# A spectral block with a gated feed-forward: lower parts and first block reordered, no moves on GpSimd's queue, second bias by a transfer

## The chip, the core and the metric

The kernel runs on one core of a Trainium2 chip. TensorE (PE) multiplies, VectorE (DVE), ScalarE (ACT) and GpSimd (POOL) work on tiles, and transfers between the chip's memory and the on-chip memory are issued by SyncE (SP) or by the queues of ACT and POOL. Each engine works through its own instructions in program order and waits where an operand isn't ready. The metric is the device time of one execution in microseconds (us); lower is better.

## What is computed

One token sequence of 4096 rows with 640 channels goes through two residual parts. In the first, a layer norm and a modulation (`sa`, `ca`, `ga`, taken from `silu(c) @ w_mod`) are followed by a real two-dimensional Fourier transform over the sequence, a two-layer block-diagonal complex network on the frequencies, a soft threshold, and the inverse transform. In the second part, a layer norm and a modulation are followed by a gated feed-forward network.

```python
    h = _layernorm(x, axis=-1) * (1 + ca) + sa
    x = x + ga * _A_ref(h, A_w1, A_b1, A_w2, A_b2)
    h = _layernorm(x, axis=-1) * (1 + cb) + sb
    x = x + gb * _B_ref(h, B_w_gate, B_w_up, B_w_down)
```

and in `_A_ref`, per frequency and for each of four blocks of 160 channels:

```python
        hr = jnp.einsum('bhwni,nio->bhwno', zr, w1[0]) - jnp.einsum('bhwni,nio->bhwno', zi, w1[1]) + b1[0]
        hi = jnp.einsum('bhwni,nio->bhwno', zi, w1[0]) + jnp.einsum('bhwni,nio->bhwno', zr, w1[1]) + b1[1]
        hr = hr * (lambda x, dt: x.astype(dt))(hr > 0, x.dtype)
...
        or_ = jnp.einsum('bhwni,nio->bhwno', hr, w2[0]) - jnp.einsum('bhwni,nio->bhwno', hi, w2[1]) + b2[0]
...
        or_ = jnp.sign(or_) * mr * (lambda x, dt: x.astype(dt))(mr > 0, x.dtype)
```

## The kernel before

The sequence is seen as 128 x 32 rows. Eight tiles `xa0` to `xa7` hold four of the 32 columns each (128 partitions x 4 x 640 numbers, 1280 KB).

**The first stage** is a loop over the tiles. `ln_stats` and `ln_apply` normalise a tile on DVE, POOL and ACT; `dft_a` (line 432) multiplies it by a 128 x 128 Fourier matrix on PE, in five matmuls `i` = 0 to 4 (the fifth takes the last 32 channels of each block); `evac_a` (line 442) copies the five results back over `xa`, on ACT, and in the last two tiles `i` = 1 and 3 on DVE; `moves` (line 366) issues what follows the tile: `write_s1(t, f)` writes the frequencies of group `f` of tile `t` to a scratch in memory, from where `load_g(ch, us)` reads a chunk of frequencies of all tiles, turned. Eight chunks `ch` are worked on one after the other. For the first chunk tiles 6 and 7 don't go through memory: `move_g(0, t, i, queue)` (line 314) moves 40 KB of row block `i` straight into the chunk's tile `g0`; `i` = 0, 1 are issued by POOL and `i` = 2, 3 by SP (lines 394 and 398). A move reads whole rows, so it needs the copy `i` and the copy of the fifth result, which comes last.

**Numbers are kept in two parts.** Matmuls run in a shortened format; a factor is split into a rounded upper part (`weights_high`, `evac_rh`, the ACT line of `evac_b`) and the rest, the lower part (`weights_low`, `evac_rl`, the DVE line of `evac_b`). `prep_weights` lists the jobs for a weight tensor: for `w1` twelve (`prep1`), of which 0, 1, 2 belong to the first 128 output columns, 6, 7, 8 to the second 128, and 3, 4, 5, 9, 10, 11 to the remaining 32 of both; for `w2` six (`prep2`, reordered in line 524).

**Between the first stage and the chunks** (lines 475 to 489): `columns` makes the modulation's columns, `ca1` is taken from it on DVE; the second bias `b2` is brought to all partitions by three matmuls (six in the trace) of ones with `b2s`, a tile that holds the bias in its first row and zeros elsewhere, and three ACT copies to `b2t`; `idle(4)` issues matmuls that nothing reads; ACT makes the upper parts of jobs 6 to 11, and DVE the lower parts of all twelve. SP then has in its queue (lines 492 to 504): the second half of the raw `w2`, eight writes to the scratch, `load_g(1)` in four pieces, `load_tb(1)`, ten more writes (tile 4 first), and small constants.

**The chunks** have four blocks `b` each. `stage_b(ch, t)` (line 594) finishes the transform with four small matmuls (eight in the trace), `evac_b` and `evac_r` scale the result by `ca1` and split it into `z` and `rz`. `stage_l1(ch, b)` (line 646) is the first layer: groups `o` = 0, `o` = 1 and a third of 32-column parts, each reading `z`, `rz` and upper and lower `w1`. `stage_l2` (line 695) is the second layer, in two halves `q`; its result gets the bias from `b2t` on DVE on its way to `tts` (line 713). A loop over positions `p` = 4·`ch` + `b` (line 837) writes the order of all of this by hand, so that the queues of the engines are fixed. Before the loop (lines 792 to 805) stand `stage_b` for (0,0), (0,4) and (0,1), the upper parts 1 and 0 of `prep2` on ACT, `evac_b` and `evac_r` of blocks 0 and 1, and the rest of `prep2`: a lower part on DVE and five operations on POOL.

**Memory.** Pool `sp` (raw `w1`, `wm1`, `b2s`, `acc0`) is left after the lower parts, and pool `hp` (`rz`, `h32`, `h`, ...) takes its place. Pool `xp` (the eight `xa`) is left after the last write is queued, and pool `p2` takes its place. `xp` holds the tiles in the order 1, 2, 3, 0, 4, 5, 6, 7 with 10,240 bytes per partition each; `p2` ends at the same edge and is one such tile longer, so that `w2b` lies where `xa1` was, `w2c` where `xa2` was, `tts` of odd chunks where `xa0` was, and `tts` of even chunks where `xa4` was. A first write there waits until the old tile has been read.

**The second part** of the kernel, the feed-forward network, follows from line 1067. Its order is made by a planner at build time from fixed costs; the change doesn't touch it.

Of the kernel before, what the change touches and what calls it, by code (L numbers as in the profile page):

```python
# [9 lines left out]
OP = mybir.AluOpType  # L10
# [163 lines left out]
def body(tc, x, w1, b1, w2, b2, wg, wu, wd, c, wm, k_fa, k_tb, k_tx, k_bm, k_bx, k_ga, k_ge, k_id, out, dbg=None):  # L174
# [27 lines left out]
    with ExitStack() as top:  # L202
# [35 lines left out]
        with ExitStack() as af:  # L238
# [97 lines left out]
            stx = ExitStack()  # L336
            xp = stx.enter_context(tc.tile_pool(name="xp", bufs=1, side="right"))
            rp = af.enter_context(tc.tile_pool(name="rp", bufs=1))
            b2t = rp.tile([P, 2, NB, BS], F32, name="b2t")
            with tc.tile_pool(name="sp", bufs=1) as sp:  # L340
                xas = []
                xts = {t: xp.tile([P, 4, D], F32, name=f"xa{t}") for t in (1, 2, 3, 0, 4, 5, 6, 7)}

                def load_x(t):
                    xa = xts[t]
                    if t < 3:
                        for i in range(4):
                            nc.sync.dma_start(xa[:, i, :], xv[:, 4 * t + i, :])
                    else:
                        nc.sync.dma_start(xa, xv[:, 4 * t:4 * t + 4, :])  # L350
                    xas.append(xa)


                def write_s1(t, f):
                    nc.sync.dma_start(s1[f][4 * t:4 * t + 4].rearrange("n r d -> r n d"),
                                      xas[t][(slice(0, 64, 4), slice(64, P, 4), slice(2, P, 4), slice(1, P, 2))[f]])

                for t in range(6):
                    load_x(t)
                wm1 = sp.tile([P, 5, D], F32, name="wm1")  # L360
                stats = {}
                pas = {}
                raws = {}


                def moves(t):
                    if t < 6:
                        write_s1(t, 0)
                    if t < 4:
                        write_s1(t, 1)  # L370
                    if t == 0:
                        load_x(6)
                        nc.sync.dma_start(c5, c)
                    elif t == 1:
                        load_x(7)
                        raws[1] = load_weights(sp, w1, "1")
                    elif t == 2:
                        nc.sync.dma_start(wm1, wm[:, 1])
                    elif t == 3:
                        load_tb(0)  # L380
                        nc.sync.dma_start(b1m, b1[:, 0:8].rearrange("p (r b) -> p r b", r=2))
                        nc.sync.dma_start(b1r, b1[0:64, 8:12])
                        nc.sync.dma_start(b2s[0:1], b2.rearrange("r b o -> (r b o)").unsqueeze(0))
                    elif t == 4:

                        load_g(0, (0, 1))
                        raws[2] = load_weights(rp, w2, "2", (0,))
                    elif t == 5:
                        for f in (2, 3):
                            write_s1(1, f)  # L390
                    elif t == 6:

                        for i in range(4):
                            move_g(0, t, i, (pool, nc.sync)[i // 2])
                        load_g(0, (2,))
                    elif t == 7:
                        for i in range(4):
                            move_g(0, t, i, (pool, nc.sync)[i // 2])


                def ln_stats(t):
                    n = 1 if t < 2 else 4
                    for i in range(0, 4, n):
                        mv, rs = layer_stats(lp, xas[t][:, i:i + n, :], n, f"a{t}_{i}")
                        nm = lp.tile([P, 4], F32, tag="nm", bufs=7, name=f"nm{t}_{i}")
                        pool.tensor_tensor(nm[:, :n], mv[:, :, 0], rs, op=OP.mult)
                        pool.tensor_tensor(nm[:, :n], nm[:, :n], mone[:, :n], op=OP.mult)
                        for k in range(n):
                            stats[t, i + k] = (mv[:, k, 0:1], rs[:, k:k + 1], nm[:, k:k + 1])

                def ln_apply(t):
                    xa = xas[t]
                    for i in range(4):
                        mean, rs, nm = stats[t, i]
                        if i >= (4, 2, 2, 3, 2, 3, 2, 1)[t]:
                            dve.tensor_scalar(xa[:, i, :], xa[:, i, :], mean, rs, op0=OP.subtract, op1=OP.mult)
                        else:
                            act.activation(xa[:, i, :], xa[:, i, :], AF.Identity, bias=nm, scale=rs)


                b2s = sp.tile([P, 2 * NB * BS], F32, name="b2s")
                pool.memset(b2s, 0.0)
                acc0 = sp.tile([P, D], F32, name="acc0")
                wx0 = sp.tile([P, P], F32, name="wx0")

                def first_scale(lo, hi):
                    if lo == 0:
                        dve.tensor_scalar(acc0, wm1[:, 0, :], sc[:, 0:1], None, op0=OP.mult)
                    for k in range(max(lo, 1), hi):
                        dve.scalar_tensor_tensor(acc0, wm1[:, k, :], sc[:, k:k + 1], acc0, op0=OP.mult, op1=OP.add)  # L430

                def dft_a(t):

                    xnr = xas[t].rearrange("p a (b e) -> p a b e", b=NB)
                    for n, i in enumerate((0, 1, 2, 3, 4) if t < 7 else (4, 0, 1, 2, 3)):
                        j = 5 * t + n
                        pa = (bank0(j // 4, [P, 512], f"pa{t}_{i}") if j % 4 == 0
                              else ps.tile([P, 512], F32, tag=f"p{j % 4}", name=f"pa{t}_{i}"))
                        mm(pa, fa, xnr[:, i, :, 0:128] if i < 4 else xnr[:, :, :, 128:160], start=True, stop=True)
                        pas[t, i] = pa  # L440

                def evac_a(t):
                    xa = xas[t]
                    for i in range(5):
                        if t > 5 and i % 2:
                            dve.tensor_copy(xa[:, i, 0:512], pas[t, i])
                        elif i == 4:
                            act.activation(xa[:, :, 512:640], pas[t, i].rearrange("p (a e) -> p a e", a=4), AF.Copy)
                        else:
                            act.activation(xa[:, i, 0:512], pas[t, i], AF.Copy)  # L450

                ln_stats(0)
                ln_stats(1)
                ln_apply(0)
                for t in range(8):
                    if t + 2 < 8:
                        ln_stats(t + 2)
                    if t + 1 < 8:
                        ln_apply(t + 1)
                    dft_a(t)  # L460
                    if t == 6:

                        prep1 = prep_weights(raws[1], w1a, w1b, w1c, True)
                        for job in prep1[:6]:
                            weights_high(*job, pool)
                        first_scale(0, 2)
                    evac_a(t)
                    if t == 6:
                        first_scale(2, 5)
                        remainders(acc0, wx0)  # L470
                    if t == 2:
                        act.activation(sc, c5, AF.Silu)
                    moves(t)

                pm1 = columns(acc0, wx0)
# [7 lines left out]
                for job in prep1[6:]:  # L483
                    weights_high(*job)
                b2v = b2t.rearrange("p r b o -> p (r b o)")
                for n, w in enumerate((512, 512, 256)):
                    act.activation(b2v[:, 512 * n:512 * n + w], pbs2[n][:, :w], AF.Copy)
                for job in prep1:
                    weights_low(*job)
# [3 lines left out]
            for t in (2, 3):  # L493
                for f in (2, 3):
                    write_s1(t, f)
# [2043 lines left out]
```

## Time and profile before

| | us |
|---|---|
| median of three runs | 1414.55 |
| lowest and highest run | 1413.67, 1416.0 |
| the profiled execution | 1411.32 |
| its span, first to last instruction | 1409.5 |

The profile is of one execution. A timeline row gives start and duration, the engine, the line of the program, the tiles written and read, how many instructions are taken together, and in brackets how long the engine sat idle before and what ended it; SPq rows are transfers issued, not their movement. PEld is the loading of a matmul's weights, which overlaps PE. A row of windows gives for each stretch of time its length and each engine's busy time with its count, then the granted clock, the busy share of the DMA engines and the data rate. A row of transfers gives how many, the KB of each, and the median time from issue to landing where the trace has it.

### The profile page before, as it was taken

How to read it: one execution, taken by the hardware profiler on the slowest of the kernel's cores; microseconds unless marked ns; L12 is line 12 of the kernel's file. 1: busy time of each engine (PE TensorE's matmuls, PEld its weight loads, DVE VectorE, ACT ScalarE, POOL GpSimd, SP SyncE). 2: the span in 40 equal slices, each digit the busy share in tenths (PEclk: the TensorE clock that was granted, in tenths of full speed). 3: DMA queues.
4: the chain of work that ended last, by engine and by line, in shares of the span. 5: the costliest groups of instructions: out<-in, count | busy, mean ns of one | idle time of the engine just before them, and what ended most of it. 6: DMA issues, size and time to landing. Idle time of an engine off the chain costs nothing. (4 is left out here: it accounts for less than half of the span.)

```text
span 1409.5 us, 23754 instructions
## 1 busy us (share of the span) xinstructions
PE 1382.5 (98%) x8410; PEld 1310.7 (93%) x8410; DVE 1067.8 (76%) x1861; ACT 765.0 (54%) x1542; POOL 604.6 (43%) x683
## 2 busy tenths in 40 slices
PE   6899999999999999999999999999999999999998
PEld 2599999967999889899999999999999999999998
DVE  8889888889888888649787668678678757375644
ACT  6879999755555554436454345546164624262341
POOL 5700200157766594326445534447153624042241
PEclk9999999999999999999999999999999999999999
DMA  9876466675998897898877998696998668956634
GB/s 371 310 244 211 157 196 193 203 232 170 327 353 308 308 335 263 293 368 308 308 225 281 375 330 288 236 326 230 375 330 309 217 218 282 350 194 217 199 115 149
DMA packets 171016, 377.34 MB, mean 268 GB/s; under 512 B 22193, under 2 KB 81649, under 8 KB 168882
## 3 DMA queue, kind: packets, MB, share of 16 engines
q1 hardware_dynamic: 161794, 359.28, 73.6%
q0 software_dynamic: 6800, 13.93, 3.1%
q10 hardware_dynamic: 2304, 2.62, 0.5%
q8 instruction: 66, 1.08, 0.3%
q14 instruction: 52, 0.43, 0.1%
HBM read 269.48 MB, written 96.80 MB: 260 GB/s over the span
## 5 line engine op out<-in xcount | busy, mean ns | idle before, releaser
L1442 DVE TENSOR_TENSOR wb<-r,wb 128x768 fp32r<-128x768 f32 (+3 forms) x170 | 170.4, 1013 | 13.5 <-ACT wb L1435 13.3
L2050 PE MATMUL pw<-h,wt 128*128 128x384 f32 x412 | 139.3, 338 | 0.6 <-ACT s_y L2069 0.6
L2052 PE MATMUL pw<-h,wt 128*128 128x384 f32 x412 | 138.3, 336 | 0.0
L2051 PE MATMUL pw<-h,wt 128*128 128x384 f32 x412 | 138.1, 335 | 0.0
L1435 ACT ACTIVATE wb<-r 128x768 fp32r<-128x768 f32 (+3 forms) x168 | 104.5, 639 | 56.3 <-PE pw L2063 41.7
L2351 PE MATMUL pc<-wq,L 128*128 128x320 f32 x846 | 132.7, 309 | 0.9 <-DMA wq<-wqd 0.9
L2110 POOL TENSOR_TENSOR sg<-s_x,sg 128x384 f32<-128x384 f32 x24 | 30.0, 1250 | 234.5 <-DVE s_x L2076 234.5
L2351 PEld LDWEIGHTS pc<-wq,L 128*128 128x128 f32 x846 | 126.3, 188 | 1.1 <-DVE x L2308 1.1
L2130 DVE TENSOR_TENSOR L<-sg,L 128x384 fp32r<-128x384 f32 x144 | 101.0, 725 | 27.7 <-ACT L L2126 27.2
L2069 ACT ACTIVATE s_x<-pw 128x384 f32<-128x384 f32 x52 | 25.6, 492 | 164.2 <-PE pw L2052 162.3
L2050 PE MATMUL pw<-h,wb 128*128 128x384 f32 x312 | 105.0, 336 | 0.0
L2051 PE MATMUL pw<-h,wb 128*128 128x384 f32 x312 | 104.4, 335 | 0.0
L2052 PE MATMUL pw<-h,wb 128*128 128x384 f32 x312 | 104.4, 335 | 0.0
L2121 POOL TENSOR_TENSOR sg<-sg,sg 128x384 f32<-128x384 f32 x72 | 91.9, 1276 | 23.4 <-DVE L L2130 20.0
L1973 PE MATMUL pg<-ht,wb 128*128 128x512 f32 x260 | 101.8, 392 | 0.0
L2351 PE MATMUL pe<-wq,L 128*128 128x320 f32 x648 | 101.7, 309 | 0.0
L1974 PE MATMUL pg<-ht,wb 128*128 128x512 f32 x260 | 101.3, 390 | 0.0
L1975 PE MATMUL pg<-ht,wb 128*128 128x512 f32 x260 | 101.2, 389 | 0.0
L2267 PE MATMUL pd<-wq,a 128*128 128x320 f32 x632 | 96.8, 310 | 0.0
L2351 PEld LDWEIGHTS pe<-wq,L 128*128 128x128 f32 x648 | 96.6, 188 | 0.0
L2267 PEld LDWEIGHTS pd<-wq,a 128*128 128x128 f32 x632 | 93.5, 188 | 0.5
L772 POOL DMA_DIRECT2D s<-co x28 | 15.7, 559 | 175.9 <-ACT co L771 175.9
(317 smaller groups left out, 3914.1 us busy)
## 6 DMA issues: line engine op xcount, KB each, us to landing
wq<-wqd SPq DMA_DIRECT2D x83, 640.0 KB, 6.1
wt<-td SPq DMA_DIRECT2D x103, 512.0 KB, 5.4
hs<-ho SPq DMA_DIRECT2D x52, 512.0 KB, 5.2
h<-hs SPq DMA_DIRECT2D x32, 768.0 KB, 7.9
td<-wt SPq DMA_DIRECT2D x25, 512.0 KB, 6.3
r<-in_B_w_gate_dram SPq DMA_DIRECT2D x24, 384.0 KB, 4.4
r<-in_B_w_up_dram SPq DMA_DIRECT2D x24, 384.0 KB, 4.3
xx<-tt SPq DMA_DIRECT2D x56, 160.0 KB, 3.3
```

The source lines that it names most:

```text
L1435: def high(ks, e=slice(0, c), copy=lambda o, i: act.activation(o, i, AF.Copy)):
L1442: dve.tensor_tensor(wbs[t, n][:, 1, ks, e], raw[t, n][:, ks, e], f32(wbs[t, n][:, 0, ks, e]), op=OP.subtract)
L1973: mm(b, wh, hh, start=(kk == 0), stop=False)
L1974: mm(b, wh, hl, start=False, stop=False)
L1975: mm(b, wl, hh, start=False, stop=(kk == 4))
L2050: mm(b, w(0, kp), a[:, kp, 0], start=start and kp == 0, stop=False, skip_group_check=not start)
L2051: mm(b, w(0, kp), a[:, kp, 1], start=False, stop=False, skip_group_check=not start)
L2052: mm(b, w(1, kp), a[:, kp, 0], start=False, stop=kp == 1, skip_group_check=not start)
L2121: pool.tensor_tensor(o, x, y, op=op)
L2130: dve.tensor_tensor(o[:, 1], raws[j], f32(o[:, 0]), op=OP.subtract)
L2267: mm(b[:, :320], l, m, start=start and i == 0, stop=stop and i == len(s) - 1)
L2351: mm(o[:, :320], ls[q][:, x, k], w[:, q, y], start=start and q == 0 and n == 0, stop=q == 1 and n == 2, skip_group_check=not start)
```

## The change

Five edits, all between the end of the first stage and the first positions of the loop.

1. **Moves.** Tiles 6 and 7 are moved by SP alone, except that `i` = 0 and 2 of tile 7 are issued by ACT. The moves stand ahead of the other transfers of their step.
2. **Raw weights.** The first half of the raw `w2` is loaded in step 5, behind the scratch writes of that step, in place of step 4.
3. **Copies of tile 7.** Only `i` = 3 stays on DVE; `i` = 1 goes to ACT.
4. **Second bias.** `b2s`, its memset, its load, its matmuls and its ACT copies go. One transfer reads the bias for each of the 128 partitions (640 KB written), behind `load_tb(1)` in SP's queue. `idle(4)` becomes `idle(6)`.
5. **Lower parts.** DVE makes the lower parts 0 to 5, then `ca1`, then (behind the definitions that are moved up) part 6, the lower parts of `z` and `rz` of block 0, then parts 7 to 11, and only then those of block 1. `rz` moves from pool `hp` to pool `lp`, as it's now written while `sp` is still in use.

```diff
                 def moves(t):
                     if t < 6:
                         write_s1(t, 0)
+                    else:
+                        for i in range(4):
+                            move_g(0, t, i, nc.scalar if t == 7 and i % 2 == 0 else nc.sync)
...
-                        nc.sync.dma_start(b2s[0:1], b2.rearrange("r b o -> (r b o)").unsqueeze(0))
                     elif t == 4:
                         load_g(0, (0, 1))
-                        raws[2] = load_weights(rp, w2, "2", (0,))
                     elif t == 5:
                         for f in (2, 3):
                             write_s1(1, f)
+                        raws[2] = load_weights(rp, w2, "2", (0,))
                     elif t == 6:
-                        for i in range(4):
-                            move_g(0, t, i, (pool, nc.sync)[i // 2])
                         load_g(0, (2,))
-                    elif t == 7:
-                        for i in range(4):
-                            move_g(0, t, i, (pool, nc.sync)[i // 2])
...
-                        if t > 5 and i % 2:
+                        if t == 6 and i % 2 or t == 7 and i == 3:
                             dve.tensor_copy(xa[:, i, 0:512], pas[t, i])
...
                 pm1 = columns(acc0, wx0)
-                dve.tensor_scalar(ca1, pm1[:, 0:5], 1.0, None, op0=OP.add)
-                pbs2 = []
-                for n, w in enumerate((512, 512, 256)):
-                    pbs2.append(ps.tile([P, 512], F32, tag="p2" if n else "p1", name=f"pb2_{n}"))
-                    mm(pbs2[n][:, :w], ones, b2s[:, 512 * n:512 * n + w], start=True, stop=True)
-                idle(4)
+                idle(6)
                 for job in prep1[6:]:
                     weights_high(*job)
-                b2v = b2t.rearrange("p r b o -> p (r b o)")
-                for n, w in enumerate((512, 512, 256)):
-                    act.activation(b2v[:, 512 * n:512 * n + w], pbs2[n][:, :w], AF.Copy)
-                for job in prep1:
+                for job in prep1[:6]:
                     weights_low(*job)
+                dve.tensor_scalar(ca1, pm1[:, 0:5], 1.0, None, op0=OP.add)
...
                 load_tb(1)
+                nc.sync.dma_start(b2t.rearrange("p r b o -> p (r b o)"),
+                                  b2.rearrange("r b o -> (r b o)").unsqueeze(0).to_broadcast([P, 2 * NB * BS]))
                 for t in (4, 0, 5, 6, 7):
                     write_s1(t, 2)
...
+                for b, tag in ((0, None), (4, None), (1, "p2")):
+                    stage_b(0, b, tag)
+                for n in (1, 0):
+                    weights_high(*prep2[n])
+                weights_low(*prep1[6])
+                evac_b(0, 0)
+                evac_r(0, 0)
+                for job in prep1[7:]:
+                    weights_low(*job)
...
+            evac_b(0, 1)
+            evac_r(0, 1)
+            weights_low(*prep2[0])
+            weights_rest(1)
+            for n in (2, 3):
+                weights_high(*prep2[n], pool)
...
-                    rzs[ch] = hp.tile([P, NB, 258], F32R, tag="rz", bufs=2, name=f"rz{ch}")
+                    rzs[ch] = lp.tile([P, NB, 258], F32R, tag="rz", bufs=2, name=f"rz{ch}")
```

The rest of the diff moves definitions and the issue of the same transfers to an earlier place in the program, in the same order.

More of the change, by code (lines that the diff above doesn't have):

```diff
@@ L506, in body @@
-            stx.close()
-            nc.sync.dma_start(idn, k_id)
-            nc.sync.dma_start(tx, k_tx)
-            p2 = af.enter_context(tc.tile_pool(name="p2", bufs=1, side="right", reuse_waits="tile"))
-            w2a = p2.tile([P, NB, 640], F32R, name="w2a")
-            w2b = p2.tile([P, NB, 640], F32R, name="w2b")
-            w2c = p2.tile([P, NB, 640], F32R, name="w2c")
-            acc = p2.tile([P, D], F32, name="acc")
-            cl = p2.tile([P, D], F32, name="cl")
-            wx = p2.tile([P, P], F32, name="wx")
@@ L518, in body @@
-            bx = p2.tile([P, 2, 128], F32, name="bx")
-            wmts = {(0, 1): p2.tile([P, D], F32, tag="wn", bufs=1, name="wm0_1")}
-            p2.tile([P, 256], F32, name="gap")
-            tts = {(1, q): p2.tile([P, 2, D], F32, tag="tu", bufs=2, name=f"tt1_{q}") for q in range(2)}
-            prep2 = prep_weights(raws[2], w2a, w2b, w2c, False)
-            prep2 = [prep2[i] for i in (0, 3, 1, 4, 2, 5)]
-            def weights_rest(n):
-                w, h, l, v, _ = prep2[n]
-                pool.tensor_tensor(w[:, :, l], v, f32(w[:, :, h]), op=OP.subtract)
@@ new lines, in body, with load_e @@
+            et = None
+            NP = 4 * NCH
+            LAST = NP - 4
+            def load_e():
+                nonlocal et
+                et = fx.tile([P, 4, D], F32, tag="gx", bufs=2, name="et")
+                nc.sync.dma_start(et.rearrange("p a b -> p (a b)"), k_ge.rearrange("p a b -> p (a b)"))
+            evac_b(0, 1)
[4 more added lines that the diff above has]
+                weights_high(*prep2[n], pool)
```

377 lines of the change are left out of this document (188 added, 189 removed).

## The prediction

> **What bounds the kernel now.** I read the page's head first, then the table of windows over the stretch that the change touches. The rows in each fence are picked from their views, not neighbours there.
>
> ```profile
> span 1409.5 us, 23754 instructions
> 55.80:60.20 4.40, 3.85 (x32) 3.70 (x33) 2.65 (x8) 2.63 (x5) 4.40 (x3) 1.00 0.95 378
> 60.20:75.40 15.20, 12.85 (x101) 12.20 (x101) 14.64 (x25) 11.47 (x26) 7.90 (x7) 1.00 0.98 361
> 75.40:262.00 186.60, 186.46 (x1456) 185.21 (x1454) 163.01 (x317) 172.68 (x355) 17.51 (x52) 1.00 0.60 193
> ```
>
> The columns of busy time are PE, PEld, DVE, ACT, POOL. From 75.4 us on PE is busy for 186.46 of 186.60 us, so whatever time PE's work there is moved by should reach the end of the kernel. From 60.2 to 75.4 it isn't PE: DVE is busy for 14.64 of 15.20 us. The start of this stretch and its end are found among PE's waits between 54 and 80 us:
>
> ```profile
> PE pb L600 <- DMA g<-xa: 1.4, 1, 1.4
> PE pc L711 <- DVE r L691: 1.1, 1, 1.1
> PE pc L711 <- DVE w2c L286: 0.5, 1, 0.5
> ```
>
> So there are two gates. The first stage_b waits for the moves, and the first second-layer block waits for DVE, whose last piece is the lower part of `w2c`. The change works on the first gate and lengthens, in part, the DVE queue that leads to the second.
>
> **First gate: the moves.** Rows of the timeline of SP, POOL, ACT, DVE and PE, and the issue-to-landing rows of single transfers (a write of tile 5, `load_g` of piece 2, the last two moves of POOL, and the page's small transfers):
>
> ```profile
> 43.67 1.95 SPq L355 DMA_DIRECT2D s<-xa  x3
> 46.65 1.61 SPq L316 DMA_DIRECT2D g<-xa  x2
> 50.14 0.53 SPq L311 DMA_DIRECT2D g<-s  x1
> 50.76 1.20 SPq L316 DMA_DIRECT2D g<-xa  x2
> 50.23 1.13 POOL L316 DMA_DIRECT2D g<-xa  x2 [0.30 <-ACT xa L448]
> 49.34 0.60 ACT L448 ACTIVATE xa<-pa 128x512 f32<-128x512 f32 x1 [0.26 <-PE pa L439]
> 49.21 1.28 DVE L446 COPY xa<-pa 128x512 f32<-128x512 f32 x2
> 55.84 2.36 PE L600 MATMUL pb<-tb,g 128*128 128x128 f32 x19 [1.43 <-DMA g<-xa]
> s<-xa SPq DMA_DIRECT2D x1, 160.0 KB, 6.4
> g<-s SPq DMA_DIRECT2D x1, 320.0 KB, 5.2
> g<-xa POOLq DMA_DIRECT2D x2, 40.0 KB, 4.8
> xx<-tt SPq DMA_DIRECT2D x56, 160.0 KB, 3.3
> ```
>
> POOL's last move is issued at about 50.23 + 1.13/2 = 50.8 and lands 4.8 later, at 55.6; PE starts at 55.84. Piece 2 of `g0` is close behind: 50.14 + 5.2 = 55.3. It's issued so late because it reads what tile 5 wrote, and that write, issued at 43.67 behind 640 KB of raw weights, lands at 43.67 + 6.4 = 50.1.
>
> With the raw weights behind it, the write of tile 5 no longer sets that time. SP issues four moves of tile 6 from 46.65 (two took 1.61, so to about 49.7 with slack in between, 49.4 without), then piece 2 at 49.4 instead of 50.14. Its landing is 49.4 + 5.2 = 54.6 with its own latency, 52.7 with the 3.3 of the small transfers. The last copy of tile 7 still ends at 49.34 + 0.60 = 49.94. DVE now has one of the two copies of 0.64, done at 49.9 too. Behind that ACT and SP issue two moves each (0.60 apiece from SP's 1.20): the last one starts at 50.6 and lands between 50.6 + 3.3 = 53.9 and 50.6 + 4.8 = 55.4. I take 54.6, where piece 2 with its own row and the middle of the moves agree. With the 0.2 from landing to PE as before, stage_b starts at 54.8: **1.0 earlier**, bounds 0.2 and 1.7.
>
> The Trainium skill (DMA: Bandwidth & Descriptors, "Issuing engines are not separate DMA queues") says that transfers of all issuing engines run on the same 16 DMA engines, and that issuing from several saves the issue time alone. By that rule the 4.8 would stay, the gain would be the 0.2 above, and this is rival C.
>
> **Second gate: DVE's queue.** What ACT, DVE and POOL do from there:
>
> ```profile
> 49.83 0.62 ACT L283 ACTIVATE w1a<-rm 128x512 fp32r<-128x512 f32 x1
> 51.79 0.30 ACT L283 ACTIVATE w1c<-rr 128x128 fp32r<-128x128 f32 x1
> 53.88 1.36 ACT L283 ACTIVATE w2a<-rm 128x640 fp32r<-128x640 f32 x2
> 54.53 0.69 DVE L286 SCALAR_TENSOR_TENSOR w1b<-rm,w1b 128x512 fp32r<-128x512 f32 x1
> 56.14 0.28 DVE L286 SCALAR_TENSOR_TENSOR w1c<-rr,w1c 128x128 fp32r<-128x128 f32 x1
> 57.73 0.75 DVE L608 SCALAR_TENSOR_TENSOR z<-pb,ca,z 128x512 fp32r<-128x512 f32 x1 [1.31 <-ACT z L607]
> 60.85 0.98 DVE L640 SCALAR_TENSOR_TENSOR rz<-pb,ca,rz 32x256 fp32r<-32x256 f32 x2 [0.23 <-ACT rz L630]
> 61.86 1.83 DVE L286 SCALAR_TENSOR_TENSOR w2a<-rm,w2a 128x640 fp32r<-128x640 f32 x1
> 65.98 1.69 DVE L286 SCALAR_TENSOR_TENSOR w2b<-rm,w2b 128x640 fp32r<-128x640 f32 x1
> 69.16 0.89 DVE L286 SCALAR_TENSOR_TENSOR w2c<-rr,sgn,w2c 128x640 fp32r<-128x640 f32 x1
> 54.71 3.11 POOL L528 TENSOR_TENSOR w2a<-rm,w2a 128x640 fp32r<-128x640 f32 x1 [3.35 <-ACT w2a L283]
> 57.80 3.59 POOL L281 TENSOR_SCALAR w2b<-rm 128x640 fp32r<-128x640 f32 x2
> 61.47 1.54 POOL L528 TENSOR_TENSOR w2b<-rm,w2b 128x640 fp32r<-128x640 f32 x1
> 65.45 1.53 POOL L528 TENSOR_TENSOR w2c<-rr,w2c 128x640 fp32r<-128x640 f32 x1
> ```
>
> *Lower parts moved.* Parts 7 to 11 ran from 54.53 to 56.42 (1.9) while DVE had time: it then waited 1.31 for `z`. Now they stand behind `rz` of block 0, in the stretch where DVE is the bound. They cost 1.9 there, less the 0.23 that DVE waited before `rz` of block 1: **1.65 later**. DVE's free time before `z` grows and isn't used. The first layer doesn't wait for them: its second group comes about 1 us after the first, in which parts 7 and 8 are made.
>
> *POOL and DVE in each other's way.* The same form, 128x640 with two operands from on-chip memory, took 1.83 and 1.69 while POOL ran its own two-operand form (61.47 to 63.0 and 65.45 to 67.0), and 0.89 with POOL free. POOL's first took 3.11, to 57.8, against 1.54: it seems to have waited out DVE's row of lower parts, which ended at 56.42. ACT's upper part of `w2a`, which releases POOL, now follows 1.2 us of issues and six parts (49.83 to 52.09: 2.26): 49.94 + 1.2 + 2.26 + 0.68 = 54.1, with the bias copies gone. There DVE is idle: parts 0 to 5 have the forms of 6 to 11, 0.6 + 1.9, so with `ca1` (0.2) and part 6 (0.6) behind its copy it's through near 53.3. So POOL needs 1.54 and is 0.6 + 1.57 = 2.2 ahead from there on. Its last operation ends near 64.8 instead of 67.0. The lower part of `w2b` then meets none, saving 0.80; that of `w2a`, which starts near 62.4, no longer meets the two-operand form but the single-operand one behind it, saving up to 0.94. I take **1.5 earlier** for both, bounds 0.8 and 1.74.
>
> Does a single-operand form of POOL hold DVE up? Two rows that overlap, from the end of the first stage:
>
> ```profile
> 47.56 1.01 POOL L281 TENSOR_SCALAR w1c<-rr,sgn 128x128 fp32r<-128x128 f32 x1
> 48.14 0.89 DVE L430 SCALAR_TENSOR_TENSOR acc<-wm,sc,acc 128x640 f32<-128x640 f32 x1
> ```
>
> DVE took its 0.89, so no. The Trainium skill (SBUF — State Buffer, "Who interferes with whom") has the pair of ports that DVE and GpSimd share as an exclusive lock, held for a whole instruction by whichever starts first. The rows of two-operand forms agree with that, the pair just quoted doesn't. By the rule, parts 7 to 11 would also wait out one of POOL's two operations of 3.59/2 = 1.80 at 57.8; this is rival D.
>
> Sum up to the second gate: −1.0 + 1.65 − 1.5 = **−0.85**.
>
> **The bias transfer.** It adds 640 KB ahead of tile 4's writes, and `tts` of chunk 0 lies where `xa4` was, so the first bias addition waits for both. The rows are the `tb(1)` load's, which precedes it, the addition, and PE's next block, which needs the addition's PSUM bank:
>
> ```profile
> tb<-in_k_tb_dram SPq DMA_DIRECT2D x1, 256.0 KB, 4.2
> 73.38 0.89 DVE L713 TENSOR_TENSOR tt<-pc,b2t 128x320 f32<-128x320 f32 x2
> 75.79 0.69 PE L711 MATMUL pc<-w2a,h 128*128 128x320 f32 x3
> 65.69 0.57 SPq L298 DMA_DIRECT2D tb<-in_k_tb_dram  x1
> ```
>
> `tb(1)` lands at 65.69 + 4.2 = 69.9. Tile 4's two writes are 960 KB; at the window's 361 GB/s they are an estimated 2.7 and land near 72.6, at the latest by 73.38, since the addition followed DVE's previous instruction directly. 640 KB more at that rate are 1.8: 74.4, at the latest 75.2. The addition would be due at 73.38 − 0.85 = 72.5, so DVE will wait some 2 us here. That is hidden as long as PE isn't reached: it needs the first of the two additions (0.45) at 75.79 − 0.85 = 74.9, and gets it at 74.4 + 0.45 = 74.85. It's just enough; at the late bound PE loses 0.7. DVE itself has room afterwards, as the windows show it with 163.01 of 186.60.
>
> **The rest at nothing:** the memset of `b2s` (POOL waits for the first statistics then), the bias matmuls (PE waits 1.4 for the moves anyway; without them it would wait longer, less two more idle ones), the bias copies (counted above), `rz` in another pool. The raw `w2` is loaded about 3 us later and is needed at 53.4; if it's late, ACT has 0.5 before the first `z` is due. The window of 75.4 to 262 uses 60% of the DMA engines, so the writes that come 1.8 later have room.
>
> **The sum:** −0.85, and nothing to half a microsecond lost at the addition: **−0.9** from the profiled execution's 1411.32, so 1410.4. That execution lies 3.2 below the median of the three runs, 1414.55; on that scale the forecast is **1413.7**.
>
> **The rivals.**
> - **A, forecast**, −2 to 0: chance 0.50.
> - **B, the bias transfer is late (slower).** One 5 KB row read 128 times may go at half the rate, and SP's stream may start later, as it now carries two more moves. The point of decision is a landing at 75.3: 0.45 later PE's block of 75.79 would start later than now. At half rate the transfer needs 3.6, tile 4 is there at 76.2, and PE starts at 76.65, 0.9 late; each further microsecond counts fully, so a transfer at a quarter of the rate (7.1) makes it 4.4. Against it: the stretch of 60.2 to 75.4 moves 361 GB/s at a busy share of 0.98, so the engines are rarely short of work. Time 1415.5, with a tail to 1419; chance 0.18.
> - **C, the start doesn't move**: the change doesn't do what it says. −0.2 + 1.65 − 1.5 = −0.05: 1414.5; chance 0.12.
> - **D, the port lock** holds for POOL's single-operand forms: −0.85 + 1.8 = +0.95: 1415.5; chance 0.08.
> - **E, more gain.** Start 1.7 earlier, no contention left (−1.74), and 1.2 of parts 7 to 11 hidden, if DVE's stretch has more slack than its busy time tells: −1.7 + 0.45 − 1.74 = −3.0: 1411.5; chance 0.12.
>
> **How the numbers follow.** A measurement of this kernel can tell about 0.2%, 2.8 us, from no change. Faster than that: the farther half of E and a little of A, 0.08. Slower: B's tail, 0.07. The same: 0.85. The range leaves out B's tail and E's far side: 1411.3 to 1416.4.
>
> **What would show it.** stage_b of block 0 starting near 54.8, on a landing; five lower parts on DVE between `rz` of block 0 and `z` of block 1; POOL's first lower part at 1.5 instead of 3.11; the lower part of `w2c` ending near 69.2 instead of 70.05; a wait of the first L713 on a transfer; PE's block of 75.79 near 74.9, and from there the same instructions at a constant shift. It's wrong if that shift isn't kept to the end, if PE waits after 75 us for `tt` or `b2t`, or if the start of stage_b hasn't moved.

## The result, and the profile after

The changed kernel takes 1425.2 us in the median of four runs, the kernel before 1415.1 on the same chip: a ratio of 1.0071, 95% interval 1.0054 to 1.0089. It is slower by 10 us, and the forecast of 1413.7 with its range up to 1416.4 is wrong. The profiled execution took 1423.76 (the one before 1411.32).

First the head of the profile after, then its table of windows over the changed stretch, cut where stage_b starts and where PE's second block of the second layer starts (columns as in the prediction: PE, PEld, DVE, ACT, POOL, then granted clock, DMA share, GB/s):

```profile
span 1422.0 us, 23727 instructions
```

```profile
55.80:64.28 8.48, 0.00 (x0) 0.00 (x1) 0.00 (x0) 1.36 (x2) 3.43 (x3) 0.51 0.89 277
64.28:86.56 22.28, 19.79 (x135) 18.86 (x136) 17.55 (x33) 14.13 (x30) 7.86 (x7) 0.88 0.96 350
86.56:262.00 175.44, 175.41 (x1373) 174.48 (x1372) 152.98 (x297) 162.36 (x334) 16.80 (x51) 1.00 0.61 199
```

For 8.48 us neither PE nor DVE does anything, and the granted clock is 0.51 in the mean. From 86.56 on PE is full, as it was before from 75.4 on. The three longest of PE's five waits of the changed kernel between 54 and 100 us, and the rows of its timeline that carry them:

```profile
PE pb L350 <- DMA g<-xa: 11.5, 1, 11.5
PE pl L668 <- DVE w1c L286: 1.3, 1, 1.3
PE pc L718 <- DVE w2c L286: 0.5, 1, 0.5
```

```profile
64.28 5.46 PE L350 MATMUL pb<-tb,g 128*128 128x128 f32 x24 [11.50 <-DMA g<-xa]
...
72.79 0.38 PE L668 MATMUL pl<-rz,w1c 128*128 128x256 f32 x1 [1.28 <-DVE w1c L286]
...
80.98 0.38 PE L718 MATMUL pc<-w2c,r 128*128 128x320 f32 x1 [0.53 <-DVE w2c L286]
...
86.56 0.69 PE L718 MATMUL pc<-w2a,h 128*128 128x320 f32 x3
```

stage_b starts 8.44 later (64.28 against 55.84), and its 24 matmuls take 5.46 instead of 2.92, 2.54 more. Together 10.98; PE's second block is 10.77 later (86.56 against 75.79), so the waits between the two cancel out to 0.2. The loss stands at the first gate, and it is two things: a late transfer, and a PE that starts slowly.

Why is the last move late? SP's own waits from 30 to 75 us, and its timeline:

```profile
SPq L415 <- DMA g<-xa: 9.2, 1, 9.2
SPq L415 <- ACT xa L501: 5.4, 2, 3.7
SPq L311 <- DMA s<-xa: 2.9, 3, 1.7
```

```profile
41.96 1.14 SPq L311 DMA_DIRECT2D g<-s  x2
52.35 1.94 SPq L415 DMA_DIRECT2D s<-xa  x3
54.33 0.63 SPq L253 DMA_DIRECT2D rm<-in_A_w_dram  x1
55.06 3.04 SPq L316 DMA_DIRECT2D g<-xa  x4
58.15 0.53 SPq L311 DMA_DIRECT2D g<-s  x1
58.77 1.20 SPq L316 DMA_DIRECT2D g<-xa  x2
```

The write of tile 5 (first of the three at L415) is issued at 52.35, where the forecast had kept 43.67. All that stands behind it on SP follows in one row: two writes, the raw weights, four moves, piece 2, two moves. The first line says what SP waited for: the landing of a *move*, `g<-xa`. But the write reads `xa5` and writes `s1`; no move of tile 7 touches either. And the only moves issued by then are ACT's two, in ACT's timeline:

```profile
50.04 1.74 ACTq L316 DMA_DIRECT2D g<-xa  x2
51.82 0.63 ACT L283 ACTIVATE w1a<-rm 128x512 fp32r<-128x512 f32 x1 [1.81 <-issue]
```

In the trace each transfer carries the semaphore that it raises on landing. SP's and ACT's transfers share eight of them (100 to 104 and 106 to 108 here) and get them in a fixed turn; GpSimd's have others (111 to 114 in the kernel before). ACT's first move has number 107. Its turn lies between the writes of tile 3 and the load of `tb`, as if it were issued there, at 36 us; the eighth transfer after it, the write of tile 5, has 107 again. The move landed at 52.28, the write was issued at 52.35. **Theory 1:** a transfer can't be issued before the one that had its semaphore is through; ACT's late move holds SP's queue by it. **Theory 2:** the loss is due to the work moved on DVE, or to the bias transfer. **Theory 3:** the write depends on the moves through its data.

### The profile page after: what moved, and what is told of

Same layout as the page of the kernel before. It is cut to its first block, busy times and chain, and to the rows that moved or that the text cites. A ratio compares the mean times of both kernels' runs of the same rounds, so it can differ in the third digit from the quotient of the medians.

```text
span 1422.0 us, 23727 instructions
## 1 busy us (share of the span) xinstructions
PE 1383.1 (97%) x8408; PEld 1312.5 (92%) x8408; DVE 1063.4 (75%) x1860; ACT 763.9 (54%) x1540; POOL 597.1 (42%) x678
```

## The experiments

Ratios are to the kernel before, run on the same chip. e1 to e4 had one chip, e5 to e8 the next, e9 to e12 the next and e13 to e15 the last, so ratios compare across these groups only as far as their intervals allow. The other columns hold, from each profile, the start of stage_b, the time of its 24 matmuls, the start of PE's second block of the second layer, and the stretches between 40 and 95 us in which the granted clock was 0.50 and not 1.00.

| kernel | ratio, 95% interval | stage_b | 24 matmuls | second block | clock 0.50 |
|---|---|---|---|---|---|
| before | 1 | 55.84 | 2.92 | 75.79 | none |
| changed | 1.0071, 1.0054 to 1.0089 | 64.28 | 5.46 | 86.56 | 55.91 to 69.57 |
| e1_all_sync | 1.0023, 1.0010 to 1.0037 | 56.61 | 4.43 | 78.65 | 56.34 to 59.75 |
| e2_before_act | 1.0068, 1.0055 to 1.0081 | 62.23 | 5.46 | 82.96 | 57.91 to 68.15 |
| e3_pool | 1.0040, 1.0024 to 1.0056 | 57.24 | 4.54 | 79.33 | 57.28 to 60.69 |
| e4_one_act | 1.0084, 1.0069 to 1.0100 | 64.73 | 4.94 | 87.02 | 55.30 to 68.95 |
| e5_after_idle | 1.0080, 1.0062 to 1.0099 | 64.34 | 2.94 | 85.16 | none |
| e6_sync_idle | 1.0008, 0.9995 to 1.0021 | 56.53 | 2.94 | 77.53 | none |
| e7_sync_lower | 1.0021, 1.0011 to 1.0031 | 56.46 | 5.43 | 78.38 | 54.88 to 61.70, 78.77 to 82.18 |
| e8_sync_idle_lower | 1.0012, 1.0002 to 1.0023 | 56.98 | 2.94 | 76.84 | none |
| e9_before_early | 0.9994, 0.9980 to 1.0008 | 53.67 | 2.84 | 74.21 | 67.44 to 70.85 |
| e10_bias_early | 0.9998, 0.9983 to 1.0012 | 56.17 | 2.94 | 74.91 | none |
| e11_all | 0.9994, 0.9980 to 1.0007 | 56.33 | 2.92 | 75.25 | none |
| e12_raw_alone | 1.0001, 0.9988 to 1.0013 | 55.84 | 2.92 | 76.93 | 69.97 to 73.38 |
| e13_after_again | 1.0080, 1.0061 to 1.0098 | 63.97 | 4.43 | 86.01 | 56.86 to 67.10 |
| e14_after_idle_again | 1.0069, 1.0049 to 1.0089 | 64.02 | 2.95 | 84.96 | 72.42 to 75.83 |
| e15_early_upper | 0.9999, 0.9985 to 1.0013 | 54.50 | 2.84 | 75.54 | 60.61 to 64.02 |

### What holds SP: e1 to e4

e1, the changed kernel with ACT's moves on SP:

```diff
-move_g(0, t, i, nc.scalar if t == 7 and i % 2 == 0 else nc.sync)
+move_g(0, t, i, nc.sync)
```

> The changed kernel with tile 7's two moves of ACT given to SP; all else of the change stays. Theory 1 (a transfer that SP issues must wait for the transfer that had its semaphore before it, ACT's move of tile 7 holds the one that tile 5's write gets, so SP stands still for 9.2 us): the write of tile 5 is issued near 43.7 instead of 52.35, SP's wait of 9.2 is gone, the last move is issued near 51.7, stage_b starts at 55.2 to 56.7 instead of 64.28, and the time is 1414.5, between 1412.5 and 1416. Theory 2 (the loss comes from what was moved on DVE, or from the bias transfer): stage_b may start near 56, but the first second-layer block stays late and the time stays above 1420. Theory 3 (tile 5's write waits for tile 7's moves because of what it reads or writes): the write stays at 52.3 or later and the time at 1425.

e2, the kernel before with ACT in GpSimd's place for tile 7, and nothing else:

```diff
 elif t == 7:
     for i in range(4):
-        move_g(0, t, i, (pool, nc.sync)[i // 2])
+        move_g(0, t, i, (nc.scalar, nc.sync)[i // 2])
```

> The kernel before with one edit: the two moves of tile 7 that GpSimd issued are issued by ACT. Theory 1: here it is the second piece of g0 (behind tile 4's write) that gets the semaphore of ACT's first move, so SP stands from about 43 to 52.4, then the raw weights, tile 5's write and piece 2 follow one after the other; stage_b starts near 64.8 instead of 55.84 and the time is 1425, between 1422 and 1428, with nothing else of the change in it. Theory 2 and theory 3: ACT's queue is as good as GpSimd's; the time stays at 1414 to 1416.5 and stage_b at 55 to 56.5.

e3, the changed kernel with `pool` in the place of `nc.scalar`:

> The changed kernel with the same two moves of tile 7 issued by GpSimd instead of ACT. Theory 1: GpSimd's transfers have semaphores of their own, so SP has no wait of 9.2; tile 5's write is issued near 43.7, stage_b starts at 54.8 to 56, time 1413.7, between 1412 and 1415.5. Theory 2: above 1420. Theory 3: as the changed kernel, 1425.

e4, the changed kernel with `nc.scalar` for `t == 7 and i == 0` alone:

> The changed kernel with only one of tile 7's moves on ACT (the first), the other on SP: the same data is moved, but one transfer fewer lies between ACT's move and the transfer that gets its semaphore next, so that is the write behind tile 5's (of tile 1, a third part). Theory 1: tile 5's write is issued near 43.7 again, SP stands from there to 52.35 at the next write, and since the moves of tile 6 stand behind it the last move still lands near 63.9; time 1424, between 1422 and 1426. Theory 3: tile 5's write itself is still issued at 52.3 or later. A theory that two moves crowd ACT's queue: half the loss goes, time 1419 to 1421.

Rows of SP's timeline in e1, in e2 and in e4:

```profile
43.59 1.94 SPq L415 DMA_DIRECT2D s<-xa  x3
45.58 0.62 SPq L253 DMA_DIRECT2D rm<-in_A_w_dram  x1
46.57 2.76 SPq L316 DMA_DIRECT2D g<-xa  x4
49.38 0.53 SPq L311 DMA_DIRECT2D g<-s  x1
50.01 2.79 SPq L316 DMA_DIRECT2D g<-xa  x4
```

```profile
41.13 11.29 SPq L311 DMA_DIRECT2D g<-s  x2
52.46 0.59 SPq L253 DMA_DIRECT2D rm<-in_A_w_dram  x1
53.16 1.92 SPq L355 DMA_DIRECT2D s<-xa  x3
```

```profile
44.18 9.86 SPq L415 DMA_DIRECT2D s<-xa  x3
54.08 0.62 SPq L253 DMA_DIRECT2D rm<-in_A_w_dram  x1
```

In e1 the three writes take 1.94 in a row from 43.59, and 6.8 of the 10 us are back. In e2 the stall stands in a kernel that has nothing else of the change, at the second of two loads of `g0` (11.29 for a pair that takes 1.14 otherwise), because there it is that load which has the semaphore of ACT's first move; nearly the whole loss is back with it (1.0068). In e4 the write of tile 5 leaves at 44.18, and the 9.86 show that the stall now lies inside the three writes: it has moved on by one transfer, as the count of eight asks. The waits of SP in e4 say the same, with the same releaser:

```profile
SPq L415 <- DMA g<-xa: 8.0, 1, 8.0
```

Theory 3 falls with e4 (the write of tile 5 doesn't wait) and e3; theory 2 as the main cause with e2. One ACT move costs as much as two. Two expectations missed: e2's stage_b came at 62.23, not 64.8, as piece 2, issued at 57.92, took 3.4 us to land there and not the 5.2 of the kernel before; and e1 and e3 stay 3.3 and 5.7 us above the kernel before, where theory 1 alone gave nothing to speak of.

### What is left without the stall: e5 to e8

e1's PE rows hold two costs that the kernel before hasn't:

```profile
56.61 4.43 PE L350 MATMUL pb<-tb,g 128*128 128x128 f32 x24 [3.97 <-DMA g<-xa]
...
64.87 0.38 PE L668 MATMUL pl<-rz,w1c 128*128 128x256 f32 x1 [1.29 <-DVE w1c L286]
```

Without the six bias matmuls PE is idle for 3.97 us, not 1.43, and then takes 1.51 more for stage_b; and it waits 1.29 for a lower part. e5 is the changed kernel with `idle(44)` for `idle(6)`; e6 is e1 with `idle(20)`:

> The changed kernel with 44 instead of 6 idle matmuls behind the column sums; nothing else. It leaves SP's wait as it is and gives PE work to do in it. Theory 1 with a clock term (the wait costs twice: 8.4 us of delay, and about 2.4 us because PE starts again at a lower clock): the write of tile 5 stays at 52.3, stage_b stays near 64.3, but its 24 matmuls take 2.9 instead of 5.46; the ratio to the kernel before goes from 1.0071 to about 1.0055 (1422.5 to 1423.5 on the scale of 1425.2). If the clock is of no account (something else is late behind stage_b): 1.0071 as it was. If idle matmuls only get in the way: above 1.008.

> The changed kernel with all moves on SP (ratio 1.0023 so far) and 20 instead of 6 idle matmuls. With SP's wait gone, PE still sits idle for 4.0 us ahead of stage_b, since the change took away the six matmuls of the bias, and its 24 matmuls took 4.43 instead of 2.92. If that is the price of the matmuls taken away, they take 2.9 here and the ratio falls by 0.0011 to 1.0012 (1.5 us); if DVE is late anyway, the ratio stays at 1.0023.

e7 is e1 with the lower parts in one row again, e8 is e7 with `idle(20)`:

```diff
-for job in prep1[:6]:
+for job in prep1:
     weights_low(*job)
...
-weights_low(*prep1[6])
 evac_b(0, 0)
 evac_r(0, 0)
-for job in prep1[7:]:
-    weights_low(*job)
```

> The changed kernel with all moves on SP, and the lower parts 6 to 11 back in front of the first z, as in the kernel before. Theory: putting them behind rz of block 0 cost 1.3 us, because PE's second group of the first layer waits for the lower part of w1c, which DVE makes in 2.04 while GpSimd runs a two-operand operation; here that wait of 1.29 is gone and the ratio falls from 1.0023 to about 1.0014. Rival, the forecast's own view: PE waits for nothing there, GpSimd's first lower part goes back to about 3 us, gets in the way of DVE's lower parts of w2a and w2b again, and the time rises by 1 us (1.003).

> Both edits of the two kernels before this one together: all moves on SP, 20 idle matmuls, lower parts 6 to 11 in front of the first z. If the two costs are separate they add: ratio 1.0023 less 0.0011 less 0.0009, about 1.0003, no difference from the kernel before; w2c's lower part then ends near 70.5 instead of 73.1. If DVE's queue takes the place of either, the ratio is no better than the better of the two.

With idle matmuls the 24 take 2.92 to 2.95 in every run. e5's ratio is still 1.0080 where 1.0055 was expected. e6 comes to 1.0008, expected 1.0012; its interval and e1's overlap. In e7 the wait for `w1c` is gone and PE goes on 2.4 earlier behind the lower part of `w2c`, but the ratio hardly moves (1.0021, not 1.0014), and in e8 the two gains don't add (1.0012, not 1.0003). e7 and e8 differ by the idle matmuls alone and ran on one chip: the means of their 11 runs each lie 1.6 us apart, with a 95% interval of 0.2 to 3.0, so their gain reaches the end. Two rows of e7, from PE's timeline and from DVE's, show what stands in the way at the second block:

```profile
78.38 0.86 PE L715 MATMUL pc<-w2a,h 128*128 128x320 f32 x3 [1.92 <-DVE tt L717]
```

```profile
77.83 0.89 DVE L717 TENSOR_TENSOR tt<-pc,b2t 128x320 f32<-128x320 f32 x2 [4.04 <-issue]
```

The first bias addition starts at 77.83, 0.18 behind the landing of tile 4's second write, which the trace has at 77.65 (in e8 76.29 and 76.11, and PE waits 0.69). That is the forecast's rival B: the bias transfer, 640 KB ahead of these writes, is hidden only while the second gate is late. The second write of tile 4 took 5.5 us from issue to landing in the kernel before (66.98 to 72.51), 10.7 in e7 and 8.9 in e8. The wait costs e7 more than its 1.92: the granted clock is 0.50 for 3.41 us behind it, and the block that takes 2.43 in the kernel before (75.79 to 78.22) takes 3.98.

### Other orders: e9 to e12, e15

e12 takes the raw weights' part of the change alone, in the kernel before: `load_weights(rp, w2, "2", (0,))` goes from the step of tile 4 to the end of that of tile 5. e9 puts it behind `b1r` instead, and `load_g(0, (2,))` from the end of tile 6's step to the end of tile 5's. e10 is e8 with the bias transfer behind the raw weights' second half. e11 joins e10 and e9's two moves, with GpSimd for ACT in tile 7 and `idle(14)`. e15 is e9 with the two upper parts of `w2a` ahead of the bias copies on ACT.

> The kernel before with one edit of the change alone: the raw weights behind the writes of tiles 5 and 1 instead of ahead of them. The forecast's first step: tile 5's write lands near 46, piece 2 is issued about 0.7 earlier, stage_b starts 0.2 to 1.7 earlier than 55.84, ratio 0.9990 to 0.9999. What the runs with all moves on SP or GpSimd suggest instead: the 640 KB now lie directly ahead of the moves, so what piece 2 gains in issue it loses in landing, stage_b starts at 55.8 to 57 and the ratio is 1.000 to 1.001.

> The kernel before with two transfers of SP moved: the raw weights of the second layer are loaded behind b1r (DMA's busy share is 0.70 from 40 to 45 us) and piece 2 of g0 is loaded right behind the three writes that follow tile 5's, ahead of the moves of tile 6. No other part of the change is in it. If the first gate is set by what lies ahead of the last moves in the DMA queues (the raw weights and piece 2, 960 KB), piece 2 lands near 50, the last move of GpSimd 1 to 2 us earlier than 55.54, stage_b starts at 53.8 to 54.8 instead of 55.84 and the time falls by 1 to 2 us (ratio 0.9990). If the moves take their 4.8 us by themselves, stage_b stays at 55.5 to 56 and the ratio at 1.000.

> The kernel with all moves on SP, 20 idle matmuls and the lower parts in front (ratio 1.0012), with the bias transfer issued right behind the second half of the raw weights instead of ahead of tile 4's two writes. In the run before this one the first bias addition started at 76.29, just behind the landing of tile 4's second write (76.11), and PE waited 0.69 for it. If the bias transfer ahead of those writes is what makes them late, tile 4's second write lands near 74.5 here, PE's wait of 0.69 is gone and the ratio falls by 0.0005 to 1.0007. If the writes are late for another reason, the wait stays.

> A version meant to beat both kernels: the kernel just before with the raw weights of the second layer loaded behind b1r, piece 2 of g0 ahead of the moves of tile 6, GpSimd in ACT's place for two moves of tile 7, and 14 idle matmuls. If both gates and the bias addition are relieved, stage_b starts at 54 to 55, the lower part of w2c ends near 68.5, and the ratio is 0.9975 to 0.999. If the moves take their time by themselves, stage_b starts near 56.5 and the ratio is 1.000 to 1.001.

> A version meant to beat both kernels: the kernel before with the two transfers of SP moved earlier (stage_b at 53.67 without a wait, ratio 0.9994), and ACT's two upper parts of w2a ahead of the three bias copies. In the run without the second edit PE stood 1.69 us for GpSimd's last lower part, which GpSimd began at 64.99 because it had got its first input only at 54.1. With the edit GpSimd begins near 52.6; the lower part of w2c on DVE becomes the last again (65.6 instead of 66.95), PE's wait of 1.69 falls to about 0.5, and its second block of the second layer comes at 72 to 73 instead of 74.21 (75.79 in the kernel before): ratio 0.9975 to 0.9985. If GpSimd's first lower part now meets more of DVE's lower parts and ends no earlier, the ratio stays at 0.9994.

e12 shows what the forecast's first step is worth without ACT: nothing at stage_b. Piece 2 is issued at 47.87 (before: 50.14) and landed at 53.15 (55.31), yet stage_b starts at 55.84 as it did, because GpSimd's last move, issued at 50.40, lands at 55.54 in spite of it. (Its second block is 1.14 late all the same; the clock is 0.50 for 3.41 us just before.) In e9, with the raw weights and piece 2 out of the way, the same move is issued at 50.21 and lands at 53.24, 3.0 instead of 5.1: the move alone doesn't take that long, what lies ahead in the DMA queues does (e11, below, doesn't fit). There stage_b no longer waits. Of the 2.17 us gained at it 1.58 are left at the second block, and the time (0.9994, with an interval that holds 1) can't tell them from nothing. PE stands for GpSimd's last lower part, and works at half the clock for 3.41 us behind that wait:

```profile
67.06 0.41 PE L711 MATMUL pc<-w2c,r 128*128 128x320 f32 x1 [1.69 <-POOL w2c L528]
```

and e15, which starts GpSimd earlier, brings GpSimd's first operation among DVE's lower parts. e15's rows of POOL and of DVE:

```profile
53.05 1.95 POOL L525 TENSOR_TENSOR w2a<-rm,w2a 128x640 fp32r<-128x640 f32 x1 [1.44 <-ACT w2a L283]
```

```profile
53.51 1.64 DVE L286 SCALAR_TENSOR_TENSOR w1a<-rm,w1a 128x128 fp32r<-128x128 f32 x1
55.08 0.80 DVE L286 SCALAR_TENSOR_TENSOR w1b<-rm,w1b 128x128 fp32r<-128x128 f32 x1
```

A lower part that took 0.29 takes 1.64, till GpSimd's operation is over (53.51 + 1.64 against 53.05 + 1.95), as the Trainium skill's exclusive lock (SBUF — State Buffer, "Who interferes with whom") has it for this form. `z` is late, PE waits 2.32 for it, and its clock is 0.50 from 60.61 to 64.02. The row behind it, 0.80 where the kernel before took 0.28, lies beside a single-operand form of GpSimd (54.98, 1.84); what held it is open. The second block came at 75.54, not at 72 to 73. In e10 tile 4's second write landed at 74.19, as expected, 6.4 us behind its issue, but the addition still started right behind it (74.37), and PE still waited 0.71. In e11 stage_b missed its 54 to 55: GpSimd's second move, issued at 50.52, landed at 56.24, beside the raw weights' second half (55.70); why it took 5.7 there and 3.0 in e9 is open. None of these five differs from the kernel before by more than its interval: no version that beats both was found.

### The clock's share: e13 and e14

The changed kernel and e5's once more, on one chip:

> The changed kernel once more, unaltered, on the chip of the two runs that follow, so that what the clock costs in the stall is a difference taken on one chip. Expected: ratio 1.0071 as before, stage_b near 64.3 with 24 matmuls in 5.0 to 5.5 us.

> The changed kernel with 44 idle matmuls, once more. In its first run stage_b's 24 matmuls took 2.94 instead of 5.46 and the step behind the lower part of w2c came 1.43 earlier (79.55 instead of 80.98), yet the ratio was 1.0080 with an interval that also holds 1.0062. If the clock costs what PE's rows say, 1.4 us reach the end: ratio 0.0010 below that of the unaltered kernel of this call. If they are lost again behind 95 us, the two ratios are equal within 0.0005.

This time the idle matmuls gain 0.0011, in the first runs they lost 0.0009; the intervals overlap in both. Windows of e13 and of e14 over the stall:

```profile
52.00:65.00 13.00, 1.74 (x12) 1.55 (x11) 1.23 (x5) 3.39 (x8) 4.46 (x3) 0.69 0.81 265
```

```profile
52.00:65.00 13.00, 9.88 (x88) 9.69 (x87) 0.93 (x3) 3.10 (x8) 4.44 (x3) 1.00 0.85 279
```

That PE's clock falls in the stall (0.69 against 1.00) and that stage_b's matmuls pay 1.5 to 2.5 us for it is shown. At the second block 1.05 of it are left (86.01 against 84.96), as e14's clock is halved later, from 72.42 to 75.83. That they reach the end isn't shown here; e7 against e8 shows it.

The same stall cost stage_b 2.54 us in the changed kernel and 1.51 in e13. The record of the granted clock tells why. Windows of the changed kernel, of e13 and of e9, cut where it changes:

```profile
55.91:69.57 13.66, 5.29 (x25) 5.29 (x26) 1.23 (x3) 2.98 (x5) 7.47 (x5) 0.50 0.94 321
```

```profile
56.86:67.10 10.24, 3.13 (x14) 3.13 (x15) 0.30 (x1) 2.05 (x3) 6.47 (x4) 0.50 0.91 311
```

```profile
64.03:67.44 3.41, 1.68 (x9) 1.19 (x9) 3.35 (x5) 3.09 (x7) 3.26 (x5) 1.00 0.83 279
67.44:70.85 3.41, 3.41 (x17) 3.41 (x16) 2.74 (x6) 0.42 (x1) 0.51 (x1) 0.50 1.00 370
```

The clock is halved in whole steps of 3.41 us: four in the changed kernel, three in e13, and one to four in each stretch of the table's last column. Of the matmuls that start at 64.28 and 63.97 the steps cover 5.29 us in the one and 3.13 in the other.

## Why the prediction was wrong, step by step

- **The first gate**, forecast at −1.0, came out at +8.44, and the failed step is "Behind that ACT and SP issue two moves each". It counted ACT's issues by their 0.6 us on ACT and took SP's queue as it was (the write of tile 5 at 43.67, no wait added there). e1 to e4 put the semaphore shared with ACT's late move in its place: SP waited 9.2 us for it. Even without that the step fails: with the raw weights behind the write alone (e12) nothing is gained, since they lie ahead of the moves now. Of the two landing times that it weighed, 3.3 and 4.8, it took the middle; the rows gave 4.3 in e1 (issued 52.25, landed 56.56) and 5.1 in e12. To that degree rival C was right; the Trainium skill's rule quoted there (DMA: Bandwidth & Descriptors, "Issuing engines are not separate DMA queues") fits e12 and e9, where the bytes ahead decide. That a second issuing engine can hold up the first is in no rival.
- **"The bias matmuls (PE waits 1.4 for the moves anyway ...)", at nothing.** They were what kept PE's clock up: without them stage_b took 1.5 us longer in e1, and e6's idle matmuls gave that back.
- **Lower parts moved, +1.65.** The size was off, and "the first layer doesn't wait for them" was wrong. Their rows in the changed kernel, DVE's and GpSimd's:

```profile
70.07 0.69 DVE L286 SCALAR_TENSOR_TENSOR w1b<-rm,w1b 128x512 fp32r<-128x512 f32 x1
70.68 2.05 DVE L286 SCALAR_TENSOR_TENSOR w1c<-rr,w1c 128x512 fp32r<-128x512 f32 x1
```

```profile
60.85 1.53 POOL L574 TENSOR_TENSOR w2a<-rm,w2a 128x640 fp32r<-128x640 f32 x1 [12.21 <-ACT w2a L283]
...
68.74 1.81 POOL L281 TENSOR_SCALAR w2c<-rr 128x640 fp32r<-128x640 f32 x1 [1.17 <-DMA s<-xa]
70.64 1.55 POOL L574 TENSOR_TENSOR w2c<-rr,w2c 128x640 fp32r<-128x640 f32 x1
```

  The five took 3.3 (70.07 to 73.36), as `w1c`'s met GpSimd's last two-operand form, and PE waited 1.28 for it.
- **POOL and DVE in each other's way, −1.5.** The mechanism was right: GpSimd's first lower part took 1.53 instead of 3.11, DVE's lower parts of `w2a` and `w2b` 0.83 and 0.80 instead of 1.83 and 1.69, 1.9 in all. But 1.37 of that were paid again at `w1c` (2.05 for 0.68): the meeting had moved, not gone.
- **The bias transfer, 0 to 0.5.** In the changed kernel it is hidden, but by the 10 us before it. With the stall gone e7 and e8 show rival B at its place, PE waiting 1.92 and 0.69, with the price that the forecast gave it (0.9) between.
- **The raw `w2`, "about 3 us later and needed at 53.4".** It landed at 60.0 and ACT waited 5.94 for it; nothing came of it only because `z` was later still.
- **Rival D** had parts 7 to 11 wait out a single-operand form of GpSimd. In the changed kernel part 7 (70.07, 0.69) lies beside one (68.74, 1.81) and took what it takes alone; in e8 the lower part of `w2a`, at 63.03, lies beside another (61.87, 1.82) and took 0.83. So no wait of 1.8 is seen. The two aren't always free of each other: GpSimd's form for `w2c` took 2.39 in the kernel before (62.98), where DVE's lower part of `w2a` ran until 63.69, and 1.81 above.

The rule that the shift at the second gate is kept to the end held roughly: over the 16 runs of the table the second block's shift, over 1413 us, stands within 0.002 of the measured ratio. That is 2.8 us, enough for the stall and too coarse for the smaller effects.

## What to carry to other kernels

Moving a transfer to another engine's queue moves more than its issue: look up in the trace which semaphore it gets and which transfers of other queues get the same one next; a late transfer that has its turn early stops a queue that has nothing to do with it. When an operation off the path is taken away, ask what it kept busy: here it was PE's clock. And a transfer or a contention that "is hidden" is hidden by something; when that goes too, it becomes the next bound (e7, e15), so gains along one path don't add up.

## What the runs showed of the hardware that was not expected

- PE's clock falls within a few microseconds of idling, in steps of 3.41 us. After 1.43 us idle (before) stage_b's 24 matmuls took 2.92, after 3.97 (e1) 4.43, after 11.5 (changed) 5.46 and after 11.27 (e13) 4.43 again, with 0.84 idle (e6) 2.94. The Trainium skill (TensorE: Matmul & The Clock Gate, "Part 1: The HAM clock gate (the "warmup" mystery)") has the clock halved after an idle window of about 3.4 us that runs freely; that the same idle time gave 5.46 once and 4.43 once agrees with a window of free phase, and so do the steps of 3.41 us that begin at 55.91 and at 56.86. But a whole window of idling isn't needed: PE was busy for 1.68 of the 3.41 us ahead of the halved step in e9 (1.80 in e12, 2.23 in e14, 1.49 in e7). How little work is enough to keep the clock up is open. PE's wait of 1.69 in e9 was thus followed by matmuls at a lower rate, in the same form as the 0.60 of the kernel before:

```profile
67.99 1.00 PE L711 MATMUL pc<-w2b,h 128*128 128x320 f32 x3
```

- The order in which semaphores are given out is neither the order in time nor that of the program's lines: ACT's move, issued at 50.04 in the step of tile 7, had its turn among transfers of tile 3's step, issued near 36 us.
- What follows the lower part of `w2c` takes 1339 us in some profiled executions and up to 1346 in others (before 1339.3, e13 1341.8, e5 1346.4) with the same work, so that 2 us at the second gate are hard to see in the time. Part of it is the clock again: in e5's profile it is 0.50 for two more steps of 3.41 us, from 335.71 and from 455.17, in the kernel before's for none from 20 us to its end. Of the 17 runs of the kernel before on e13's chip the fastest (1408.59) has a mean granted clock of 1.000, the slowest (1418.41) of 0.996.
